# A first unit of 128 rows, the weights split over fewer attention steps, and their sign taken on VectorE instead of GpSimd

## The chip, the cores and the metric

One core of one Trainium2 chip runs the whole program. The time is device microseconds of one launch; the kernel before takes 1611.05 us (median of 3 runs, 1611.02 to 1611.76). The engines are named as in the profile: PE (TensorE matmuls), PEld (its weight loads), DVE (VectorE), ACT (ScalarE), POOL (GpSimd), SP (SyncE, which issues the DMAs here).

## What is computed

Attention with a top-32 mask over 8 batches, 8 heads, 576 positions and a head size of 64, then a gated feed-forward part over the 4608 rows that come out:

```
scores = q @ k^T / 8                       # per batch and head, 576 x 576
kth    = 32nd largest of each row
attn   = softmax of the scores >= kth      # the others are dropped
x      = (attn @ v) as 4608 x 512          # 8 heads of 64 side by side
out    = (sigmoid(x @ w_gate) * (x @ w_val)) @ w_out    # d_ff = 1536
```

q, k and v are 32-bit floats. [...]

## The kernel before, in words

**Attention.** The work is cut into 160 steps. A step (loop variable `n` in `run`) is one tile of 128 query rows for a pair of heads; the last 64 rows of a batch are a narrow step in which the two heads share one tile. So a step has two halves of 128 rows, a narrow one has one: 36 halves a batch, 288 in all. Each half goes through PE (scores, L192), ACT (L199 to SBUF), DVE (`cand`, L257: the 8 largest of each of 8 segments, then four kinds of small operations L261, L263), ACT and POOL (L269, L275: scores under a lead value), DVE (`kths`, L285: the threshold), ACT (L206: exponentials), DVE (L211: mask and sum), PE (L297: transposes into `pt`; `weigh`, L316 to L327: times v). ACT and POOL also split keys, queries and the result (L158, L160, L173, L174, L340, L341) into two parts.

**Groups and units.** `groups` lists the order of the tiles: (batch, first tile, end), each for four pairs of heads. In batch 0 it is tiles 0 and 1 for four pairs (8 steps), tiles 2 and 3 (8 steps), and the 64 rows left (4 steps). `units` lists how the rows are cut for the feed-forward part, as (first row, rows): three units of 256 rows, then ten of 384. A unit may begin when all its rows have come out of the attention; `todo` then gets a generator `ffn` that yields after each piece. A unit runs over three groups of the hidden size (`order`): four pieces of 24 matmuls (`pz`, L369 to L371), then four of 12 (`po2`, L388 to L390; a profile shows it as `po`). That is 432 matmuls a unit whatever its rows, and 18 weight tiles of 1 MB.

**The split of the weights.** 18 weight tiles in 36 halves. Each half (`split_weights`) is loaded (`wraw`, L125), the upper word is scaled on ACT (L132), two POOL instructions multiply the upper word by zero so that only its sign is left (L134), and three DVE instructions (L135, L138, L139) make the high part and the fraction. Then ACT (L140), three matmuls into `wrest` (L141 to L143) and ACT again (L144) make the low part, and L145 stores both to DRAM, from where later units load them. The first unit takes group 1, then 2, then 0, since the tiles of groups 1 and 2 can be used as they are made (`fresh`).

**Pace.** While the split runs, `due` says how many of the 36 halves must have been issued by step `n`: 20 halves over the first `SOON` = 8 steps, then, once the first unit is ready, the other 16 up to step `RUSH` = 15; pieces of the first unit go between them. After that `MILES`, pairs of (attention rows done, feed-forward rows done), sets the pace: at 512 attention rows 256 feed-forward rows, and so on, up to a distance of 448 rows that is kept to the end. Within this a scheduler puts each engine's instructions in order; each engine then runs its own list strictly in order.

## Time and profile before

| what | value |
|---|---|
| median of 3 runs | 1611.05 us |
| the profiled execution | 1610.83 us, of which 1609.0 us are the span of its instructions |
| PE busy | 1541.2 us (96%) |
| DVE, POOL, ACT busy | 1310.4, 1162.1, 1122.6 us |
| HBM read and written | 316.0 and 28.3 MB |

In the 40 slices of the span PE begins with 5778889 and stays at 9 from then on, while DVE and POOL read 7 to 9 in the first seven slices: the start is one stage, with the split in it, the long middle another, and the last three slices, in which DVE reads 2, 0 and 1 and little but feed-forward matmuls is left, a third. PE's busy time is no measure of its speed: matmuls overlap, so their rate has to be read from the distance between their starts.

### The profile page before, as it was taken

The page shows a single profiled execution, that of the slowest core. Times are in us where ns is not written, and L with a number is a line of the kernel's source. Part 1 is how long each engine was busy: PE and PEld are TensorE (multiplying, and loading weights), DVE is VectorE, ACT ScalarE, POOL GpSimd, SP SyncE. Part 2 cuts the span into 40 slices and gives each one's busy share as a digit, 9 for nine tenths or more (in the row PEclk, how much of TensorE's full clock was granted, in tenths as well). Part 3 has the DMA queues.
Part 4 walks back from the last instruction along what each step waited for, and adds up shares of the span by engine and source line. Part 5 has one row for each costly group of instructions (what it writes and reads, how often), then busy time and mean ns, then how long its engine had stood idle before and what let it go on. Part 6 is the DMA issues. An engine that isn't in the chain of part 4 may idle for free.

```text
span 1609.0 us, 34312 instructions
## 1 busy us (share of the span) xinstructions
PE 1541.2 (96%) x10586; PEld 1402.2 (87%) x10586; DVE 1310.4 (81%) x5859; ACT 1122.6 (70%) x2531; POOL 1162.1 (72%) x1871
## 2 busy tenths in 40 slices
PE   5778889999999999999999999999999999999998
PEld 3446669999999999989999999999999999999998
DVE  7999889788998889898888889888988888888201
ACT  7788767677877677777677767678677777767221
POOL 8999998668776886688767876688766887665211
PEclk9789899999999999999999999999999999999999
DMA  7656578777755665565555565566564665554574
GB/s 243 198 175 196 195 253 320 291 273 285 268 185 190 226 233 189 179 234 193 203 207 180 205 235 196 213 213 213 197 219 164 238 215 195 206 200 175 175 281 162
DMA packets 92066, 346.66 MB, mean 215 GB/s; under 512 B 10208, under 2 KB 37344, under 8 KB 63456
## 3 DMA queue, kind: packets, MB, share of 16 engines
q1 hardware_dynamic: 91872, 344.37, 61.7%
q8 instruction: 86, 1.41, 0.4%
q14 instruction: 108, 0.88, 0.2%
HBM read 316.01 MB, written 28.31 MB: 214 GB/s over the span
## 4 chain that ended last, share of the span: by engine, by line
PE 82%; DVE 6%; POOL 4%; ACT 4%; DMA 2%; issue 2%; SPq 0%; POOLq 0%; ACTq 0%; DVEq 0%
PE pz L369 12%; PE pz L370 12%; PE pz L371 12%; PE pss L192 9%; PE po L316 6%; PE pt L297 6%; PE po L388 6%; PE po L389 6%; PE po L390 6%; PE po L318 2%; DMA wraw<-in_w_dram 2%; POOL u L275 2%; DVE cand L257 1%; PE po L327 1%; PE po L321 1%
## 5 line engine op out<-in xcount | busy, mean ns | idle before, releaser
L275 POOL TENSOR_TENSOR u<-s,under 128x288 f32<-128x288 f32 x576 | 454.1, 810 | 108.8 <-ACT under L269 96.1
L257 DVE MAX8 cand<-s 128x8 f32<-128x72 f32 x2304 | 348.8, 218 | 73.3 <-ACT s L199 71.8
L369 PE MATMUL pz<-xh,w 128*128 128x384 f32 (+1 forms) x1184 | 393.4, 333 | 0.7 <-ACT xh L340 0.7
L371 PE MATMUL pz<-xh,w 128*128 128x384 f32 (+1 forms) x1184 | 388.8, 328 | 0.0
L370 PE MATMUL pz<-xl,w 128*128 128x384 f32 (+1 forms) x1184 | 388.3, 328 | 0.4 <-POOL xl L341 0.3
L211 DVE SCALAR_TENSOR_TENSOR e<-s,kths,e 128x576 f32<-128x576 f32 x288 | 281.1, 980 | 10.0 <-ACT e L206 9.8
L269 ACT ACTIVATE under<-s,leads 128x576 bf16<-128x576 f32 x288 | 223.0, 775 | 90.4 <-DVE leads L261 51.0
L285 DVE MAX8 kths<-u 128x8 f32<-128x584 f32 x288 | 218.9, 760 | 39.9 <-POOL u L276 38.6
L377 POOL TENSOR_TENSOR gl<-gf,gh 128x384 fp32r<-128x384 f32 (+1 forms) x156 | 157.6, 1011 | 121.1 <-ACT gh L376 117.3
L206 ACT ACTIVATE e<-s,st 128x576 f32<-128x576 f32 x288 | 209.4, 773 | 28.1 <-POOL st L265 27.9
L369 PEld LDWEIGHTS pz<-xh,w 128*128 128x128 f32 x1184 | 223.0, 189 | 1.9 <-ACT xh L340 1.2
L370 PEld LDWEIGHTS pz<-xl,w 128*128 128x128 f32 x1184 | 223.4, 189 | 0.9 <-POOL xl L341 0.9
L371 PEld LDWEIGHTS pz<-xh,w 128*128 128x128 f32 x1184 | 223.2, 189 | 0.0
L192 PE MATMUL pss<-k,qh 128*128 128x288 f32 (+2 forms) x672 | 198.3, 313 | 23.7 <-ACT s L199 15.3
L199 ACT ACTIVATE s<-pss 128x576 f32<-128x576 f32 x288 | 185.1, 643 | 47.3 <-PE pss L192 42.8
L298 ACT ACTIVATE et<-pt 128x384 f32<-128x384 f32 x384 | 179.0, 487 | 39.8 <-PE pt L297 39.1
L389 PE MATMUL po<-gl,w 128*128 128x384 f32 (+1 forms) x592 | 194.5, 331 | 0.1
L390 PE MATMUL po<-gh,w 128*128 128x384 f32 (+1 forms) x592 | 192.3, 327 | 0.0
L388 PE MATMUL po<-gh,w 128*128 128x384 f32 (+1 forms) x592 | 190.0, 336 | 0.0
L297 PE MATMUL pt<-ident,e 128*128 128x128 f32 x1152 | 180.3, 276 | 7.5 <-DVE e L211 5.3
L192 PE MATMUL pss<-k,ql 128*128 128x288 f32 (+2 forms) x672 | 184.7, 296 | 0.0
L297 PEld LDWEIGHTS pt<-ident,e 128*128 128x128 f32 x1152 | 142.6, 142 | 21.0 <-DVE e L211 8.8
(97 smaller groups left out, 3307.2 us busy)
## 6 DMA issues: line engine op xcount, KB each, us to landing
w<-ws SPq DMA_DIRECT2D x222, 1024.0 KB, 4.9
v<-in_v_dram SPq DMA_DIRECT2D x68, 352.0 KB, 3.9
qraw<-in_q_dram SPq DMA_DIRECT2D x160, 128.0 KB, 3.2
kraw<-in_k_dram SPq DMA_DIRECT2D x64, 288.0 KB, 3.8
wraw<-in_w_dram SPq DMA_DIRECT2D x36, 512.0 KB, 4.4
ws<-w_split SPq DMA_DIRECT2D x36, 512.0 KB, 4.2
out_dram<-acc SPq DMA_DIRECT2D x40, 192.0 KB, 5.0
out_dram<-acc SPq DMA_DIRECT2D x12, 128.0 KB, 5.3
```

Source lines behind the costliest of these rows:

```text
L192: nc.tensor.matmul(ps[:, half, o : o + n], x[:, h * P : (h + 1) * P], ks[h][:, k0 : k0 + n], start=t == 0, stop=t == len(todo) - 1,)
L211: nc.vector.scalar_tensor_tensor(e[:, j], s[:, j], kth[j], e[:, j], op0=ALU.is_ge, op1=ALU.mult, accum_out=st[:, 4 + j : 5 + j])
L257: nc.vector.max(cand[:, j, 8 * g : 8 * g + 8], s[:, j, g * SEG : (g + 1) * SEG])
L269: nc.scalar.activation(under[:, j], s[:, j], AF.Sign, bias=bound, scale=-CUT, accum_out=sums[:, j : j + 1])
L275: nc.gpsimd.tensor_tensor(u[:, j, part], s[:, j, part], under[:, j, part], op=ALU.mult)
L297: nc.tensor.transpose(pt[:, c], ef[:, k0 : k0 + P], ident)
L369: nc.tensor.matmul(ps, wt[:, u, 0, d], xh, start=d == 0, stop=False)
L370: nc.tensor.matmul(ps, wt[:, u, 0, d], xl, start=False, stop=False)
L371: nc.tensor.matmul(ps, wt[:, u, 1, d], xh, start=False, stop=d == NP - 1)
L388: nc.tensor.matmul(ps, wt[:, e % 2, 0, f], gh, start=f == 0, stop=False)
L389: nc.tensor.matmul(ps, wt[:, e % 2, 0, f], gl, start=False, stop=False)
L390: nc.tensor.matmul(ps, wt[:, e % 2, 1, f], gh, start=False, stop=f == FG - 1)
```

## The change

The first unit has 128 rows, the second 256 and all others 384; batch 0 is taken as tile 0 (4 steps), tiles 1 and 2 (8 steps), tile 3 with the 64 rows left (8 steps). `SOON` is 6 and `RUSH` 10, with the line of `due` moved by one step; `MILES` has two entries. In the split the two POOL instructions go; DVE shifts the lead by itself (a new instruction) and then takes the sign bit straight from the upper word. The number of units (13), of matmuls in them and of weight loads stays.

```diff
-    units = [(2 * P * i, 2 * P) for i in range(3)]
-    units += [(t, U) for t in range(2 * U, B * S, U)]
+    units = [(0, P), (P, 2 * P)]
+    units += [(t, U) for t in range(U, B * S, U)]
     halves = {0: ((0, 3), (3, NT + 1)), 1: ((0, 2), (2, NT + 1))}
-    groups = [(0, 0, 2), (0, 2, NT), (0, NT, NT + 1)]
+    groups = [(0, 0, 1), (0, 1, NT - 1), (0, NT - 1, NT + 1)]
...
-    SOON, RUSH = 8, 15
+    SOON, RUSH = 6, 10
...
-    MILES = [(512, 256), (832, 512), (1152, 768), (1536, 1152), (1984, 1536)]
+    MILES = [(384, 128), (832, 384)]
...
                     nc.scalar.activation(lead, sign, AF.Copy, scale=2.0**-112)
-                    for part in (slice(0, 2 * P), slice(2 * P, 4 * P)):
-                        nc.gpsimd.tensor_scalar(sign[:, part], sign[:, part], 0.0, None, op0=ALU.mult)
+                    nc.vector.tensor_scalar(lead_u, lead_u, 3, None, op0=ALU.logical_shift_left)
                     nc.vector.scalar_tensor_tensor(
-                        lead_u, lead_u, 3, top, op0=ALU.logical_shift_left, op1=ALU.bitwise_or
+                        lead_u, top, 0x80000000, lead_u, op0=ALU.bitwise_and, op1=ALU.bitwise_or
                     )
...
-                    due = HELD if not todo else HELD + (2 * n_w - HELD) * (n - SOON) // (RUSH - SOON)
+                    due = HELD if not todo else HELD + (2 * n_w - HELD) * (n + 1 - SOON) // (RUSH - SOON)
```

From the split on every line number is one lower in the changed kernel. The order of the instructions shows what it does to three places.

ACT at the start of the program, before; `wt_lead_0_0` is the first weight half, `s_0_0_0` the first scores:

```order
L158 ACTIVATE k_0_0_1_155<-kraw_0_0_1_153 128x576
L173 ACTIVATE qh_0_1_0_161<-qraw_0_1_0_159 128x256
L132 ACTIVATE wt_lead_0_0_305<-wraw_0_0_303 128x512
L199 ACTIVATE s_0_0_0_177<-pss_0_0_0_0_178 128x576
L132 ACTIVATE wt_lead_0_1_322<-wraw_0_1_320 128x512
```

The same place of the changed kernel:

```order
L157 ACTIVATE k_0_0_1_155<-kraw_0_0_1_153 128x576
L172 ACTIVATE qh_0_0_1_161<-qraw_0_0_1_159 128x256
L198 ACTIVATE s_0_0_0_189<-pss_0_0_0_0_190 128x576
L132 ACTIVATE wt_lead_0_0_319<-wraw_0_0_317 128x512
L172 ACTIVATE qh_0_0_2_179<-qraw_0_0_2_177 128x256
```

The first scores now leave ACT before the first weight half, and no longer behind it.

DVE at the end of the split, before (`17_1` is the last weight half; `kths<-u_0_4_2` and `e_0_4_2` belong to the narrow step of the third pair, `1_0_0` and `1_1_0` to batch 1):

```order
L285 MAX kths_121<-u_0_4_2_3158 128x8
L215 RECIPROCAL st_0_4_1_3056<-st_0_4_1_3056 128x1
L261 MAX tops_1_0_0_3365<-cand_1_0_0_3364 128x8 x2
L394 SCALAR_TENSOR_TENSOR acc_0_1_0_1753<-po2_0_2_0_2627,acc_0_1_0_1753 128x256
L263 MATCH_REPLACE cand_1_0_0_3364<-tops_1_0_0_3365,cand_1_0_0_3364 128x64
L394 SCALAR_TENSOR_TENSOR acc_0_1_1_1768<-po2_0_2_1_2641,acc_0_1_1_1768 128x256
L263 MATCH_REPLACE cand_1_0_0_3364<-tops_1_0_0_3365,cand_1_0_0_3364 128x64
L211 SCALAR_TENSOR_TENSOR e_0_4_2_3157,st_0_4_2_3155<-s_0_4_2_2970,kths_121,e_0_4_2_3157 128x576
L261 MAX tops_1_0_0_3365<-cand_1_0_0_3364 128x8 x2
L135 SCALAR_TENSOR_TENSOR wt_lead_17_1_2675<-wt_lead_17_1_2675,wraw_17_1_2673 128x512
```

The same place of the changed kernel, with the new shift L133:

```order
L284 MAX kths_121<-u_0_4_1_2885 128x8
L332 TENSOR_TENSOR rs_0_2_3_2752<-po_0_2_3_2740,rs_0_2_3_2752 128x256
L138 SCALAR_TENSOR_TENSOR wt_frac_16_1_2044<-wraw_16_1_2041 128x512
L214 RECIPROCAL st_0_3_1_2778<-st_0_3_1_2778 128x2
L260 MAX tops_0_3_2_3032<-cand_0_3_2_3031 128x8
L134 SCALAR_TENSOR_TENSOR wt_lead_17_0_2088<-wraw_17_0_2086,wt_lead_17_0_2088 128x512
L374 SCALAR_TENSOR_TENSOR gf_0_2_3_2019<-gf_0_2_3_2019,pz_0_2_3_1_2006 128x128
L210 SCALAR_TENSOR_TENSOR e_0_4_1_2884,st_0_4_1_2882<-s_0_4_1_2676,kths_121,e_0_4_1_2884 128x576
L133 TENSOR_SCALAR wt_lead_17_1_2104<-wt_lead_17_1_2104 128x512
```

The last half now stands behind fewer attention halves. Counted in the lists up to the last `wt_frac`: 35 of L285 and L211 before and 30 now, 320 of L257 before and 264 now, 113 of L261 and 76 of L263 before and 96 and 64 now.

PE around the last `wrest`, before:

```order
L390 MATMUL po2_0_2_2_2690<-gh_0_2_3_2471,w_split_17_2655 128x256
L142 MATMUL wrest_17_1_2677<-w_split_17_2655,minus_299 128x512
L388 MATMUL po2_0_2_3_2704<-gh_0_2_0_2075,w_split_17_2655 128x256
L389 MATMUL po2_0_2_3_2704<-gl_0_2_0_2076,w_split_17_2655 128x256
L143 MATMUL wrest_17_1_2677<-wt_frac_17_1_2676,plus_298 128x512
L321 MATMUL po_0_4_1_3315<-et_0_4_1_3303,v_2_1_3033 64x64
```

The same place of the changed kernel:

```order
L301 MATMUL pt_0_4_1_0_3240<-ident_105,e_0_4_1_2884 128x128
L140 MATMUL wrest_17_1_2106<-wt_lead_17_1_2104,ident_105 128x512
L141 MATMUL wrest_17_1_2106<-w_split_17_2085,minus_313 128x512
L142 MATMUL wrest_17_1_2106<-wt_frac_17_1_2105,plus_312 128x512
L301 MATMUL pt_0_4_1_0_3240<-ident_105,e_0_4_1_2884 128x128
L387 MATMUL po2_0_2_2_2118<-gh_0_2_0_1601,w_split_17_2085 128x128
```

In both, PE has then done two of the three groups of the first unit but for a few matmuls; that unit has 256 rows before and 128 now.

## Rows read from the trace of the kernel before

**Rows 1.** Windows: stretch, its length, each engine's busy time (instructions), clock, DMA.
```profile
17.00:178.00 161.00, 121.48 (x598) 82.18 (x598) 155.82 (x625) 126.72 (x267) 151.79 (x196) 0.87 0.59 193
178.00:244.00 66.00, 56.60 (x330) 41.90 (x330) 54.98 (x176) 49.40 (x110) 63.42 (x85) 0.91 0.76 248
244.00:300.00 56.00, 56.00 (x481) 52.98 (x480) 48.88 (x240) 39.56 (x97) 40.47 (x76) 0.99 0.85 318
500.00:1500.00 1000.00, 998.68 (x6979) 935.08 (x6977) 857.77 (x3940) 729.02 (x1653) 731.07 (x1219) 1.00 0.59 204
```

**Rows 2.** Waits of DVE from 10 to 178 us: total, times, longest.
```profile
DVE cand L257 <- ACT s L199: 12.7, 3, 10.7
DVE kths L285 <- POOL u L276: 2.2, 2, 1.3
```

**Rows 3.** Waits of DVE from 178 to 244 us.
```profile
DVE cand L257 <- ACT s L199: 3.7, 3, 2.0
DVE kths L285 <- POOL u L276: 2.8, 1, 2.8
DVE rs L333 <- ACT rs L330: 2.6, 1, 2.6
```

**Rows 4.** Timeline around 243 us: start, duration, the last instruction of the split on DVE.
```profile
242.91 1.08 DVE L139 SCALAR_TENSOR_TENSOR wt_frac<-wraw 128x512 fp32r<-128x512 uint32 x1
```

**Rows 5.** Matmul distances: window of 384-row matmuls alone, then timeline with 256 rows.
```profile
1530.00:1590.00 60.00, 60.00 (x345) 59.52 (x345) 7.59 (x14) 12.42 (x25) 10.15 (x10) 1.00 0.74 272
...
249.36 0.28 PE L369 MATMUL pz<-xh,w 128*128 128x256 f32 x1
...
250.56 0.28 PE L370 MATMUL pz<-xl,w 128*128 128x256 f32 x1
```

**Rows 6.** Groups by line from 500 to 1500 us: count, busy us, mean ns, idle before.
```profile
L369 PE MATMUL pz<-xh,w 128*128 128x384 f32 x783 | 269.2, 345 | 0.5 <-ACT xh L340 0.5
...
L389 PE MATMUL po<-gl,w 128*128 128x384 f32 x400 | 136.6, 342 | 0.1
...
L211 DVE SCALAR_TENSOR_TENSOR e<-s,kths,e 128x576 f32<-128x576 f32 x200 | 198.7, 998 | 7.6 <-ACT e L206 7.5
L285 DVE MAX8 kths<-u 128x8 f32<-128x584 f32 x198 | 150.7, 761 | 27.2 <-POOL u L276 26.2
```

**Rows 7.** Groups by line on DVE from 0 to 244 us.
```profile
L257 DVE MAX8 cand<-s 128x8 f32<-128x72 f32 x320 | 49.5, 216 | 16.6 <-ACT s L199 16.4
L211 DVE SCALAR_TENSOR_TENSOR e<-s,kths,e 128x576 f32<-128x576 f32 x35 | 34.4, 987 | 0.0
L135 DVE SCALAR_TENSOR_TENSOR wt_lead<-wt_lead,wraw 128x512 uint32<-128x512 uint32 x36 | 32.1, 893 | 0.8 <-POOL wraw L134 0.8
L139 DVE SCALAR_TENSOR_TENSOR wt_frac<-wraw 128x512 fp32r<-128x512 uint32 x36 | 30.1, 836 | 0.2
L285 DVE MAX8 kths<-u 128x8 f32<-128x584 f32 x35 | 26.5, 757 | 5.2 <-POOL u L276 5.1
L138 DVE TENSOR_SCALAR wraw<-wt_lead 128x512 uint32<-128x512 uint32 x36 | 22.7, 630 | 0.1
L261 DVE MAX8 tops<-cand 128x8 f32<-128x64 f32 x77 | 15.5, 211 | 0.4
```

**Rows 8.** Instructions on `wraw`: count, duration ns min/median/max, first and last start.
```profile
L134 POOL TENSOR_SCALAR wraw<-wraw x72: 872/902/1819, 10.2 to 238.4; 128x256 f32<-128x256 f32 x72
...
L135 DVE SCALAR_TENSOR_TENSOR wt_lead<-wt_lead,wraw x36: 669/886/1283, 14.1 to 240.7; 128x512 uint32<-128x512 uint32 x36
L138 DVE TENSOR_SCALAR wraw<-wt_lead x36: 402/583/1024, 15.0 to 242.0; 128x512 uint32<-128x512 uint32 x36
L139 DVE SCALAR_TENSOR_TENSOR wt_frac<-wraw x36: 667/754/1285, 16.4 to 242.9; 128x512 fp32r<-128x512 uint32 x36
```

**Rows 9.** Timeline of the start: ACT's first weight half and first scores.
```profile
9.43 0.66 ACT L132 ACTIVATE wt_lead<-wraw 128x512 f32<-128x512 f32 x1 [3.45 <-DMA wraw<-in_w_dram]
```

**Rows 10.** Waits of ACT from 0 to 244 us.
```profile
ACT wt_lead L132 <- DMA wraw<-in_w_dram: 15.8, 15, 3.5
```

## What the change should do to the time

> **What bounds the kernel now.** I read the windows by stage first, then the waits, then single groups. From 500 to 1500 us PE is busy for 998.7 of 1000 us and DVE for 857.8; from 244 to 300 us PE is already busy without a gap [rows 1]. So from the moment the weights are split, every microsecond is PE work, and the time is (end of the split) + (PE work still to do then). The split's last DVE instruction ends at 242.91 + 1.08 = 244.0 us [rows 4].
>
> Before that PE is not the limit: it has gaps, and its clock is 0.87 and 0.91 of full [rows 1]. From 17 to 178 us DVE is busy 155.8 of 161 us and POOL 151.8; DVE's real waits in that stretch, apart from the 10.7 us at the program's start, are 2.0 + 2.2 = 4.2 us [rows 2]. DVE sets the pace there. From 178 to 244 us POOL is busy 63.4 of 66 us and DVE only 55.0, and DVE's waits go back to results that others owe it: scores, `u` of POOL, `rs` [rows 1, 3]. There POOL is the fullest engine and DVE loses 11 us. So the stage of 244 us holds 155.8 + 55.0 + about 6 (its part before 17 us, after the 10.7) = 216.9 us of DVE work.
>
> The forecast needs two numbers for the changed kernel: when the split ends, and how much less PE has done by then.
>
> **When the split ends.** DVE's list is strictly in order, so its last split instruction comes no sooner than the work ahead of it. Counted in the lists, there are 56 MAX8 of `cand` less ahead of it (at 49.5 / 320 = 0.155 us, 8.7 us), 5 of L285 and 5 of L211 less (0.757 + 0.987 us each pair, 8.7 us), 29 small operations of 64 columns less (0.21 us as L261, 6 us) [rows 7], and about 3 us less in narrower results (my estimate from eight L333 and eight L375 that halve or shrink). That is 26.4 us. Instructions overlap at their ends: the busy times of all DVE groups of this stretch add up to 253 us for an engine that is busy 216.9, so each price counts 0.86: 23 us.
>
> Added are 36 shifts, one for each half. None is in the trace. The nearest row is L138, also a one-tensor integer operation over 512 columns: 402 to 1024 ns, mean 630 [rows 7, 8]. At the mean it is 36 x 0.630 x 0.86 = 19.5 us; the ends are 12.4 us (all at 402) and 31.7 us (all at 1024). I take the mean. The rewritten L135 reads the same two tensors as before and keeps its price.
>
> The 72 POOL instructions that go (902 ns median [rows 8]) free about 65 us of POOL. POOL had no time left from 178 to 244 us; without them it is no longer the fullest engine. What does that give DVE? First, the 11 us of waits can go. Second, DVE's own instructions may get shorter: L135, L138 and L139 have means of 893, 630 and 836 ns and minima of 669, 402 and 667 [rows 7, 8], so something lengthens them, and POOL is the suspect. From below: nothing is gained, since L211 takes 987 ns on average in the split's stage with POOL 94% busy and 998 ns later with POOL 73% busy [rows 1, 6, 7]. From above: all three fall to their minima, (224 + 228 + 169) ns x 36 x 0.86 = 19 us. L211 is the nearer row, since it shows the same kind of operation at two loads of POOL; but the POOL work that goes is not of the kind that stays. I take 7 us.
>
> The Trainium skill, page "SBUF — State Buffer", section "Who interferes with whom", states a stricter rule: GpSimd and VectorE share one pair of ports under an exclusive lock, and a VectorE instruction with two SBUF inputs, or a one-source one in its two-port mode, waits for the whole of a GpSimd instruction that reads SBUF. By that rule 72 holders of the lock go and the upper end is the right one; that L211 is as long at 73% as at 94% speaks against taking it in full. It is the second rival below.
>
> So DVE's work ahead of the last split instruction is 216.9 - 23 + 19.5 - 7 = 206.4 us. It starts a little earlier: the first scores sat on ACT behind the first weight half, which waited 3.45 us for its DMA and ran from 9.43 us on [rows 9]; now they go first, but DVE's second instruction is a shift that needs that same half. Eight MAX8 come out ahead, 1.2 us: the start is 9.5 us instead of 10.7. Waits: 4.2 us as in the stretch where DVE sets the pace. The split ends at 9.5 + 206.4 + 4.2 = 220.1 us, 23.9 us sooner.
>
> **What PE still has to do.** The rest after the split is larger, and this is what the change pays with. Feed-forward: two thirds of the first unit are done by then, 170.7 rows before and 85.3 now, so 85.3 more rows remain. 345 matmuls of 384 rows take 60 us, 174 ns each; at 256 rows ten distances are 1.20 us, 120 ns each [rows 5]. 432 matmuls of 174 ns for 384 rows are 0.196 us a row: 16.7 us. Narrow matmuls are dearer by the row; of those with 128 rows (66 ns on the line through 120 and 174; no row shows any) only the last third of the unit falls after the split, 144, and they cost about 1 us more than their share. Feed-forward: 17.5 us.
>
> Attention: 5 halves fewer have passed DVE. From 500 to 1500 us there are 198 halves and about 3 x 783 + 3 x 400 = 3549 feed-forward matmuls [rows 6]; at 174 ns these take 618 us, which leaves 382 us, or 1.93 us of PE for a half. PE's own list has a little more than 5 halves less in scores, transposes and products, in all 11 us.
>
> Nothing else changes in the PE-bound part: the same 13 units, the same matmuls, the same distance of 448 rows at the end and so the same tail. One risk was that DVE bounds the next stretch, since `MILES` lets only 256 feed-forward rows go with 448 attention rows. But up to 832 rows there are then 22 halves left, 22 x 1.93 + 10 + 52 (last third of the first unit, and 432 x 120 ns) = 104 us of PE, against 22 x 857.8 / 198 = 95 us of DVE [rows 1, 6]. PE stays the limit, by a tenth.
>
> **Sum.** -23.9 + 17.5 + 11 = +4.6 us on the profiled execution's 1610.83 us, which is within 0.3 us of the median 1611.05: 1615.4, rounded to 1615 us. The shorter split is worth nearly as much as it costs; the sign of the result hangs on DVE's prices.
>
> **Rivals.**
> Forecast, 1615 us, its own range 1609 to 1623 (shift between 402 and 800 ns, relief between 3 and 10 us): the split ends near 220 us with DVE full. Chance 0.63.
>
> DVE runs free, 1596 us: without the POOL instructions the three old split operations fall to their minima (19 us instead of 7) and the shift costs 402 ns (7 us less), so the split ends at 201 us. For it: the minima exist, and POOL is full in the whole stage [rows 1, 8]. Against: L211 is no shorter with POOL at 73% [rows 6, 7], and `u`, keys and queries stay on POOL. Chance 0.22.
>
> The split gets a new wait, 1631 us, slower: 36 halves in ten steps instead of 15 ask more of the chain DMA, ACT, DVE for each half with three raw buffers; ACT already waits 15.8 us for `wraw` in 15 places [rows 10]. If DVE then idles in the second half of the split as it did from 178 to 244 us (11 of 66 us, so 18 us in 110) in place of 2 us, the split ends at 236 us. It decides as soon as a raw half lands later than DVE reaches its shift. Against: the load's buffer comes free at L139, several us of other DVE work before the next half. Chance 0.15.
>
> **How the numbers follow.** A measurement of this kernel can tell 0.2%, 3.2 us, from no change, so "same" is 1607.8 to 1614.3. The forecast's own range gives some 0.05 faster, 0.20 same and 0.38 slower; the free DVE counts as faster but for 0.02, the new wait as slower: faster 0.25, same 0.22, slower 0.53. The range from 1601 to 1631 holds the forecast and half of each rival.
>
> **What would show it.** In the profile after: the last `wt_frac` at about 220 us; PE without gaps right after it; DVE over 95% busy from 17 us to there, with next to no waits for POOL; POOL at 60 to 70% there; 30 of L285 by then; the shift near 0.6 us and L135, L138, L139 a little shorter; the same rate of halves from 500 us on, and an equal tail. I am wrong if the split ends before 214 us (faster) or after 232 us, if L135 or L211 fall near their minima, or if PE shows gaps after the split, since then the rest is not PE's.

## The result, and the profile after

The changed kernel takes 1631.8 us (median of 4 runs, 1630.1 to 1633.0) against 1611.4 us for the kernel before on the same chip: ratio 1.0128 (1.0113 to 1.0143), 20 us slower. Its profiled execution is 1631.1 us, with a span of 1628.9 against 1609.0 us.

The windows of the four stretches of [rows 1], in the kernel after:

```profile
17.00:178.00 161.00, 129.38 (x607) 91.09 (x607) 152.22 (x587) 124.03 (x265) 102.19 (x143) 0.80 0.63 211
178.00:244.00 66.00, 63.46 (x460) 53.41 (x456) 60.62 (x233) 48.46 (x114) 50.45 (x77) 0.92 0.83 293
244.00:300.00 56.00, 56.00 (x493) 52.97 (x493) 38.71 (x184) 36.28 (x88) 29.69 (x54) 1.00 0.78 286
500.00:1500.00 1000.00, 1000.00 (x6970) 937.21 (x6967) 848.98 (x3943) 730.95 (x1652) 729.11 (x1218) 1.00 0.59 205
```

POOL falls from 151.8 to 102.2 and from 63.4 to 50.5 us, and PE bounds the long middle as before. The last split instruction on DVE, the counterpart of [rows 4], in the timeline:

```profile
216.62 1.19 DVE L138 SCALAR_TENSOR_TENSOR wt_frac<-wraw 128x512 fp32r<-128x512 uint32 x1
```

It ends at 217.8 us; 220.1 was predicted, 244.0 was it before. On PE the split's last matmul, in the timelines of after and of before:

```profile
223.74 0.40 PE L142 MATMUL wrest<-wt_frac,plus 128*128 128x512 f32 x1
```

```profile
246.28 0.40 PE L143 MATMUL wrest<-wt_frac,plus 128*128 128x512 f32 x1
```

So PE leaves the split at 224.1 instead of 246.7 us, 22.5 us sooner, and yet the kernel is slower: what is left to do then takes 42.5 us more. The groups of DVE from 0 to 244 us, which answer to [rows 7]; L133 is the new shift:

```profile
L256 DVE MAX8 cand<-s 128x8 f32<-128x72 f32 x296 | 46.6, 218 | 8.1 <-ACT s L198 8.1
L210 DVE SCALAR_TENSOR_TENSOR e<-s,kths,e 128x576 f32<-128x576 f32 x35 | 32.8, 940 | 0.0
L138 DVE SCALAR_TENSOR_TENSOR wt_frac<-wraw 128x512 fp32r<-128x512 uint32 x36 | 29.8, 829 | 0.3
L134 DVE SCALAR_TENSOR_TENSOR wt_lead<-wraw,wt_lead 128x512 uint32<-128x512 uint32 x36 | 28.9, 804 | 0.1
...
L133 DVE TENSOR_SCALAR wt_lead<-wt_lead 128x512 uint32<-128x512 uint32 x36 | 19.8, 553 | 6.3 <-ACT wt_lead L132 6.2
L137 DVE TENSOR_SCALAR wraw<-wt_lead 128x512 uint32<-128x512 uint32 x36 | 18.5, 517 | 0.1
```

The means of the three old operations are lower than before, L134 by 89 ns, L137 by 113, L138 by 7, and still far from the minima. Their medians are not (count, duration ns min/median/max; 886, 583 and 754 before [rows 8]):

```profile
L134 DVE SCALAR_TENSOR_TENSOR wt_lead<-wraw,wt_lead x36: 668/690/1287, 10.8 to 212.1; 128x512 uint32<-128x512 uint32 x36
L137 DVE TENSOR_SCALAR wraw<-wt_lead x36: 406/428/1018, 13.3 to 215.0; 128x512 uint32<-128x512 uint32 x36
L138 DVE SCALAR_TENSOR_TENSOR wt_frac<-wraw x36: 666/688/1289, 14.6 to 216.6; 128x512 fp32r<-128x512 uint32 x36
```

So most of them run near the minimum, and some take nearly twice as long. Now the matmuls of the first unit, in the timeline of PE; first a piece after the split, then one inside it (start, duration):

```profile
228.20 0.28 PE L368 MATMUL pz<-xh,w 128*128 128x128 f32 x1
228.31 0.27 PE L369 MATMUL pz<-xl,w 128*128 128x128 f32 x1
228.43 0.27 PE L370 MATMUL pz<-xh,w 128*128 128x128 f32 x1
...
229.54 0.30 PE L296 MATMUL pt<-ident,e 128*128 128x128 f32 x1
```

```profile
130.07 0.41 PE L368 MATMUL pz<-xh,w_split 128*128 128x128 f32 x1
130.29 0.41 PE L369 MATMUL pz<-xl,w_split 128*128 128x128 f32 x1
130.50 0.41 PE L370 MATMUL pz<-xh,w_split 128*128 128x128 f32 x1
```

From 228.20 to 229.54 us there are 12 distances of 112 ns; the median over such stretches is 111 ns. The prediction had 66. A matmul of 128 rows costs nearly as much as one of 256, 120 ns [rows 5]. Inside the split the distance is 213 ns. Windows of smaller stretches show the clock there, and where else PE loses time:

```profile
100.00:120.00 20.00, 14.78 (x69) 8.38 (x68) 20.00 (x79) 17.43 (x37) 12.26 (x19) 0.93 0.58 191
120.00:140.00 20.00, 19.52 (x84) 18.22 (x84) 20.00 (x86) 13.45 (x32) 11.64 (x18) 0.50 0.51 165
140.00:160.00 20.00, 20.00 (x89) 14.36 (x89) 14.76 (x48) 7.44 (x17) 9.75 (x16) 0.67 0.38 121
160.00:180.00 20.00, 20.00 (x133) 15.74 (x132) 18.87 (x63) 19.39 (x43) 13.64 (x18) 1.00 0.78 252
...
330.00:360.00 30.00, 26.45 (x185) 21.72 (x181) 27.13 (x134) 23.16 (x53) 25.05 (x44) 1.00 0.54 173
```

From 120 to 140 us the granted clock is 0.50, the level of 1.2 GHz, with PE busy for 19.5 of 20 us; from 140 to 160 us PE is the limit, and DVE has 5 us of gaps in a stretch that should be DVE's. From 330 to 360 us it is the other way round: PE has gaps of 3.5 us at full clock, in what the prediction took for PE-bound. From 300 to 500 us they are 5.0 us; before, 1.4:

```profile
300.00:500.00 200.00, 194.96 (x1372) 177.90 (x1372) 177.09 (x842) 151.21 (x344) 152.73 (x254) 1.00 0.60 207
```

```profile
300.00:500.00 200.00, 198.61 (x1578) 185.61 (x1578) 170.88 (x815) 147.09 (x347) 145.87 (x253) 1.00 0.71 252
```

(after, then before). From 224 us to the end of the program the gaps are 5.0 us, before 2.7 from 246.7 us on.

### The profile page after: what moved, and what is told of

The parts are those of the page before. It is cut to its first block, busy times and chain, and to the rows that moved or that the text cites. A ratio compares the mean times of both kernels' runs of the same rounds, so it can differ in the third digit from the quotient of the medians.

```text
span 1628.9 us, 34375 instructions
## 1 busy us (share of the span) xinstructions
PE 1574.1 (97%) x10658; PEld 1434.8 (88%) x10658; DVE 1315.0 (81%) x5899; ACT 1130.1 (69%) x2539; POOL 1098.2 (67%) x1803
## 4 chain that ended last, share of the span: by engine, by line
PE 76%; POOL 1%; DVE 1%; ACT 0%; issue 0%; POOLq 0%; ACTq 0%
PE pz L369 11%; PE pz L370 11%; PE pz L368 11%; PE pss L191 8%; PE pt L296 6%; PE po L315 6%; PE po L387 6%; PE po L388 5%; PE po L389 5%; PE po L317 2%; PE po L326 1%; PE po L320 1%; PE pt L301 1%; POOL u L274 1%; PE po L322 0%
## 5 line engine op out<-in xcount | busy, mean ns | idle before, releaser
L368 PE MATMUL pz<-xh,w 128*128 128x384 f32 (+2 forms) x1184 | 399.9, 338 | 0.0
L370 PE MATMUL pz<-xh,w 128*128 128x384 f32 (+2 forms) x1184 | 394.2, 333 | 0.0
L369 PE MATMUL pz<-xl,w 128*128 128x384 f32 (+2 forms) x1184 | 392.8, 332 | 0.7 <-POOL xl L340 0.7
L210 DVE SCALAR_TENSOR_TENSOR e<-s,kths,e 128x576 f32<-128x576 f32 x288 | 277.3, 967 | 0.2
L376 POOL TENSOR_TENSOR gl<-gf,gh 128x384 fp32r<-128x384 f32 (+2 forms) x156 | 154.9, 994 | 112.9 <-ACT gh L375 108.9
L198 ACT ACTIVATE s<-pss 128x576 f32<-128x576 f32 x288 | 184.6, 641 | 39.6 <-PE pss L191 38.7
L387 PE MATMUL po<-gh,w 128*128 128x384 f32 (+2 forms) x592 | 195.6, 342 | 1.0 <-DVE acc L393 0.8
L388 PE MATMUL po<-gl,w 128*128 128x384 f32 (+2 forms) x592 | 196.0, 334 | 0.0
L389 PE MATMUL po<-gh,w 128*128 128x384 f32 (+2 forms) x592 | 194.9, 332 | 0.0
```

The costliest lines, as they stand in the source:

```text
L210: nc.vector.scalar_tensor_tensor(e[:, j], s[:, j], kth[j], e[:, j], op0=ALU.is_ge, op1=ALU.mult, accum_out=st[:, 4 + j : 5 + j])
L368: nc.tensor.matmul(ps, wt[:, u, 0, d], xh, start=d == 0, stop=False)
L369: nc.tensor.matmul(ps, wt[:, u, 0, d], xl, start=False, stop=False)
L370: nc.tensor.matmul(ps, wt[:, u, 1, d], xh, start=False, stop=d == NP - 1)
L387: nc.tensor.matmul(ps, wt[:, e % 2, 0, f], gh, start=f == 0, stop=False)
L388: nc.tensor.matmul(ps, wt[:, e % 2, 0, f], gl, start=False, stop=False)
```

## The experiments

Every ratio is to the kernel before on the same chip. It takes 1610.1 to 1611.4 us on the chips used, so a difference between the times of two other kernels is good to about 2 us. Unless said otherwise an edit is against the changed kernel.

The table divides the span of some of the kernels, in us. Each PE instruction after PE has left the split counts from its start to the start of the next one; idle time stands apart as gaps.

| kernel | PE leaves the split at | feed-forward | attention | gaps | span |
|---|---|---|---|---|---|
| before | 246.7 | 914.0 | 445.6 | 2.7 | 1609.0 |
| changed | 224.1 | 941.6 | 458.2 | 5.0 | 1628.9 |
| experiment 1 ("kernel 1") | 232.0 | 917.3 | 445.1 | 4.9 | 1599.2 |
| experiment 2 | 240.4 | 955.3 | 455.5 | 4.1 | 1655.3 |
| experiment 5 | 220.8 | 963.2 | 454.5 | 0.9 | 1639.4 |
| experiment 6 | 224.0 | 966.8 | 458.5 | 4.6 | 1653.8 |
| experiment 9 | 237.9 | 934.4 | 454.1 | 11.5 | 1637.9 |
| experiment 10 | 269.2 | 897.6 | 440.7 | 10.1 | 1617.7 |

**1. The new split alone.** The kernel before with only the four lines of the split changed.

```diff
-                    for part in (slice(0, 2 * P), slice(2 * P, 4 * P)):
-                        nc.gpsimd.tensor_scalar(sign[:, part], sign[:, part], 0.0, None, op0=ALU.mult)
+                    nc.vector.tensor_scalar(lead_u, lead_u, 3, None, op0=ALU.logical_shift_left)
...
```

> The kernel before with the new split alone (shift and sign on VectorE, no GpSimd), old units, groups and pace. Theory A (the narrow unit is what costs): the shift adds some 17 us to VectorE up to the end of the split, shorter split operations and the waits for GpSimd from 178 to 244 us give back 10 to 18 us, the split ends between 240 and 248 us, and the time is 1607 to 1615 us, no change that 0.2% can tell. Rival B (the work moved to VectorE is what costs): VectorE is the limit of the whole split and gets nothing back, the split ends at 255 us or later, and the time is 1622 us or more.

1601.1 us, 0.9945 (0.9928 to 0.9962): faster than either theory said. Windows of this kernel:

```profile
17.00:178.00 161.00, 127.24 (x617) 86.54 (x618) 158.93 (x636) 130.34 (x275) 105.80 (x148) 0.86 0.61 199
...
178.00:244.00 66.00, 56.94 (x390) 45.00 (x389) 64.31 (x226) 51.17 (x115) 55.80 (x80) 0.97 0.83 278
...
300.00:500.00 200.00, 198.31 (x1569) 184.88 (x1569) 178.76 (x858) 154.23 (x359) 152.53 (x260) 1.00 0.69 242
```

DVE has 36 shifts more (20.6 us) and is done with the split at 229.1 instead of 244.0 us, with 34 halves of attention done by then instead of 35: it is busy 64.3 instead of 55.0 of the 66 us from 178 on [rows 1]. Up to the last split instruction DVE is busy for 217.3 us, before for 216.9; but after its first instruction it idles 2.5 us instead of 16.4. What GpSimd's 72 instructions cost was above all VectorE's waits.

**2. The rest alone.** The changed kernel with the old split on GpSimd (the same lines, the other way).

> The changed kernel with the old split: two GpSimd instructions a half, no shift on VectorE; units of 128, 256, 384 rows and the new pace stay. Theory A: the narrow unit is still there, so the time stays well above before; GpSimd is full again, and the split ends at 225 to 235 us instead of 218, so the time is 1635 to 1645 us. Rival B (the new split costs the time): without the shift VectorE has 17 us less to do, and the time falls back to 1615 us or less.

1658.8 us (1641.4 to 1663.5), 1.0277 (1.0209 to 1.0344). Units and pace without the new split lose more than the whole change, and the split gains in both surroundings. Neither theory goes as high; the split ends on DVE at 237.4 us, later than the first one said. Windows here:

```profile
240.00:260.00 20.00, 20.00 (x97) 19.24 (x97) 12.95 (x66) 6.92 (x19) 10.58 (x21) 0.50 0.47 172
260.00:300.00 40.00, 40.00 (x258) 38.30 (x258) 9.92 (x35) 9.76 (x27) 10.66 (x21) 0.69 0.67 237
```

Behind the split PE is full here at a granted clock of 0.50 and 0.69, while DVE is busy for 13 of 20 and 10 of 40 us. In the changed kernel the clock is 1.00 there. The 154 narrow matmuls that are left take 33 us, in the changed kernel 168 take 20.

**3. GpSimd back in every second half** (against kernel 1).

```diff
+                    if i == 0:
                         nc.vector.tensor_scalar(lead_u, lead_u, 3, None, op0=ALU.logical_shift_left)
...
+                    else:
+                        for part in (slice(0, 2 * P), slice(2 * P, 4 * P)):
+                            nc.gpsimd.tensor_scalar(sign[:, part], sign[:, part], 0.0, None, op0=ALU.mult)
...
```

> Old units, groups and pace; every first half takes the new split (shift on VectorE), every second half the old one (two GpSimd instructions). VectorE then has 18 shifts less, some 9 us, than with the new split alone (1601 us, split ends at 229 us), and GpSimd some 32 us more, which still leaves it room. If VectorE's list alone sets the end of the split: it ends at 220 to 224 us and the time is 1592 to 1597 us. Rival (GpSimd's instructions lengthen VectorE's by as much as is saved): 229 to 234 us, and 1601 to 1606 us.

1609.2 us, 0.9986 (0.9977 to 0.9996): 8 us worse than kernel 1, with 18 shifts fewer on DVE, and worse than the rival too. Its last split instruction in the timeline, and its window:

```profile
236.68 0.67 DVE L145 SCALAR_TENSOR_TENSOR wt_frac<-wraw 128x512 fp32r<-128x512 uint32 x1
```

```profile
178.00:244.00 66.00, 55.71 (x353) 44.24 (x353) 59.96 (x214) 50.67 (x114) 61.00 (x81) 0.95 0.76 247
```

The split ends 8.2 us later than in kernel 1, with one half of attention more done by then (35, some 4 us of DVE), and DVE has 4.4 us more gaps from 178 to 244 us, with POOL at 61 of 66 us. That GpSimd's instructions lengthen the stage is shown.

**4. The pace: `MILES`, `SOON` and `RUSH`, then all of it** (with `RUSH` 14).

```diff
-    MILES = [(384, 128), (832, 384)]
+    MILES = [(384, 128), (832, 384), (1152, 768), (1536, 1152), (1984, 1536)]
```

> The changed kernel, but after 832 attention rows the pace of the kernel before (768 feed-forward rows at 1152, 1152 at 1536, 1536 at 1984) instead of a distance of 448 rows at once. Theory A: the 5 us in which PE is idle between 300 and 500 us come from the pace, since feed-forward matmuls are held back there; they go, and the time is 1625 to 1628 us. Rival: PE waits there for the attention itself (masks of VectorE, products of GpSimd), the gaps only move, and the time stays within 3 us of 1631.

```diff
-    SOON, RUSH = 6, 10
+    SOON, RUSH = 8, 15
```

> The changed kernel with the pace of the split from before (20 halves over 8 steps, the rest up to step 15); units of 128, 256, 384 rows, groups and new split stay. Theory A (the narrow unit costs): most of the loss stays, 1618 to 1632 us. Rival B (the shorter pace costs): the time falls to 1601 to 1610 us, near the 1601 us of the new split with old units and pace.

```diff
-    SOON, RUSH = 6, 10
+    SOON, RUSH = 8, 14
-    MILES = [(384, 128), (832, 384)]
+    MILES = [(512, 256), (832, 512), (1152, 768), (1536, 1152), (1984, 1536)]
-                    due = HELD if not todo else HELD + (2 * n_w - HELD) * (n + 1 - SOON) // (RUSH - SOON)
+                    due = HELD if not todo else HELD + (2 * n_w - HELD) * (n - SOON) // (RUSH - SOON)
```

> The changed kernel (new split, first unit of 128 rows) with all of the pace of before: SOON 8, RUSH 14 and the five MILES. Theory A (the pace is not the cause: alone, its two parts made the changed kernel 5 us slower each): 1632 to 1642 us. Rival (the two parts of the pace belong together, and the new one costs the 11 us that the narrow unit does not): 1618 to 1624 us.

1636.5 us, 1.0163 (1.0146 to 1.0180); 1637.0 us, 1.0152 (1.0135 to 1.0169); 1657.6 us, 1.0281 (1.0217 to 1.0346). The old pace is worse in every form, and worst in full, each time beyond what either theory gave. The new pace is not the cause of the loss; with this narrow unit the old one costs 5 us in each part and 26 us in full. In both runs with the old pace of the split PE is full from 240 to 260 us at a granted clock of 0.50, with DVE busy for 6 of 20 us, as in experiment 2.

**5. A second narrow unit.** The third unit, 384 rows, cut into 128 and 256.

```diff
-    units += [(t, U) for t in range(U, B * S, U)]
+    units += [(3 * P, P), (4 * P, 2 * P)]
+    units += [(t, U) for t in range(2 * U, B * S, U)]
```

> The changed kernel with the third unit (384 rows) cut into 128 and 256: a second unit of 128 rows, all of it after the split, where every microsecond is PE work. 432 matmuls of 128 rows and 432 of 256 take the place of 432 of 384. Theory A (a matmul of 128 rows takes as long as its weight load, 111 ns): 48.0 + 51.8 - 75.2 = 24.6 us more, so 1652 to 1660 us. Rival (66 ns, on the line through 120 ns at 256 rows and 174 ns at 384, as the prediction had it): 28.5 + 51.8 - 75.2 = 5.1 us more, so 1634 to 1640 us.

1643.6 us, 1.0215 (1.0195 to 1.0235), 12 us over the changed kernel: between the two. Its matmuls of 128 rows are 111 ns apart, and feed-forward takes 21.6 us more (table), near theory A. But PE has hardly any gaps from 300 to 500 us (0.7 instead of 5.0 us), the split ends 3.3 us sooner on PE, and attention takes 3.7 us less. The place was not clean.

**6. The last unit cut** into 256 and 128 rows, where PE has little else to do.

```diff
+    units[-1:] = [(B * S - U, 2 * P), (B * S - P, P)]
```

> The changed kernel with its last unit of 384 rows cut into 256 and 128, in the stretch in which PE has little but feed-forward matmuls left. Theory A (a matmul of 128 rows costs 111 ns, one of 256 rows 120, one of 384 rows 174, and all of it is paid where PE is the limit): 432 x (0.111 + 0.120 - 0.174) = 24.6 us more, 1656 us (1653 to 1659). Theory B (the prediction's line through 120 and 174 down to 66 ns; the 111 ns come from something at the start of the program): 432 x 0.012 = 5.2 us more, 1637 us (1635 to 1639).

1656.0 us, 1.0288 (1.0270 to 1.0305): 24.2 us more, where theory A had 24.6. In the table feed-forward takes 25.2 us more and the rest is as in the changed kernel. The last unit in the timeline:

```profile
1630.44 0.27 PE L389 MATMUL po<-gl,w 128*128 128x128 f32 x1
1630.55 0.27 PE L390 MATMUL po<-gh,w 128*128 128x128 f32 x1
1630.66 0.28 PE L388 MATMUL po<-gh,w 128*128 128x128 f32 x1
```

Where PE is the limit the 111 ns are paid in full. The granted clock is 1.00 from 1600 to 1650 us.

**7. A lean first unit**: of the three products with a weight (high x high, high x low, low x high) only the first, 144 instead of 432 narrow matmuls; two thirds of that unit's products are left out.

```diff
...
-                        nc.tensor.matmul(ps, wt[:, u, 0, d], xl, start=False, stop=False)
-                        nc.tensor.matmul(ps, wt[:, u, 1, d], xh, start=False, stop=d == NP - 1)
+                        if n > P:
+                            nc.tensor.matmul(ps, wt[:, u, 0, d], xl, start=False, stop=False)
+                            nc.tensor.matmul(ps, wt[:, u, 1, d], xh, start=False, stop=d == NP - 1)
...
```

> The changed kernel, but the first unit (128 rows) takes only the product high x high: 144 matmuls of 128 rows instead of 432, the others left out. Theory A, strong form (the narrow unit is PE's limit inside the split too, where the trace of the changed kernel shows PE full from 120 to 180 us at a clock of 0.5 to 0.67): some 20 us inside the split and 96 x 0.111 = 11 us behind it go, so 1598 to 1606 us. Weak form (inside the split PE is hidden behind VectorE): only the 11 us behind the split go, 1619 to 1624 us. Rival B (the shorter pace is what costs, not the unit): 1627 us or more.

1613.3 us, 1.0017 (1.0008 to 1.0027): 18.5 us under the changed kernel, between the two forms of theory A; rival B is out. The 288 matmuls are 32 us at 111 ns; a part of them lies beside DVE's work in the split. Clock from 120 to 160 us: 0.76 and 0.93.

**8. The same matmuls twice as wide.** The first unit takes its 128 columns twice; the copy is not used.

```diff
+        twice = n == P
...
+        def wide(x):
+            return x.unsqueeze(1).to_broadcast([P, 2, P]) if twice else x
...
-                        nc.tensor.matmul(ps, wt[:, u, 0, d], xh, start=d == 0, stop=False)
+                        nc.tensor.matmul(to, wt[:, u, 0, d], wide(xh), start=d == 0, stop=False)
...
```

> The changed kernel, but the 432 matmuls of the first unit take their 128 columns twice (256 columns; the second copy is not used). Theory A (narrow matmuls cost their weight load, 111 ns, and besides bring the granted clock down where they run back to back): the clock from 120 to 160 us is above 0.85 instead of 0.50 and 0.67, the matmuls there are 120 to 140 ns apart instead of 213, the time is 1620 to 1628 us although PE does twice the columns. Theory B (the clock falls there for another reason, and only the distance counts): the clock stays at 0.5 to 0.7, the distance grows from 111 to 120 ns at full clock and from 213 to about 240 ns at the low one, and the time is 1636 to 1641 us (432 x 9 ns = 4 us, and some 200 x 27 ns = 5 us).

1632.7 us, 1.0138 (1.0121 to 1.0155): within the changed kernel's interval. Of theory A the clock came true, the time did not:

```profile
120.00:140.00 20.00, 20.00 (x137) 17.75 (x137) 20.00 (x90) 16.55 (x39) 12.69 (x21) 0.86 0.52 176
140.00:160.00 20.00, 18.92 (x122) 14.64 (x121) 20.00 (x70) 16.48 (x39) 17.52 (x24) 1.00 0.55 184
```

With distances of 120 ns and DVE full again, the whole is as long as before. The clock has to be read in finer windows, first of the changed kernel, then of this one:

```profile
126.00:153.00 27.00, 27.00 (x109) 23.20 (x109) 25.25 (x100) 15.01 (x36) 19.19 (x29) 0.50 0.34 107
```

```profile
126.00:153.00 27.00, 26.41 (x189) 22.58 (x188) 27.00 (x115) 23.79 (x57) 22.25 (x30) 1.00 0.55 183
```

From 110 to 119 us the clock is 1.00 and 0.99 with PE busy for 4.0 and 5.4 of 9 us, and from 119 to 126 us it is 0.50 and 0.53: it falls at the same place in both kernels. With 128 columns it stays at 0.50 up to 153 us, with 256 columns it is back at 1.00 from 126 us on. Narrow matmuls do not always go with the low clock: behind the split they run at 1.00 in the changed kernel (224 to 244 us), and so they do in experiment 6.

Nor is the low clock where the 20 us went: with 432 x 9 ns = 4 us more of PE's work and the same time, it was worth some 3 us here. That is an estimate, since the order moved too: the split ends at 225.4 us with 33 halves done, in the changed kernel at 217.8 with 30.

**9. The narrow unit second**, with the pace of before (against kernel 1).

```diff
-    units = [(2 * P * i, 2 * P) for i in range(3)]
-    units += [(t, U) for t in range(2 * U, B * S, U)]
+    units = [(0, 2 * P), (2 * P, P)]
+    units += [(t, U) for t in range(U, B * S, U)]
-    groups = [(0, 0, 2), (0, 2, NT), (0, NT, NT + 1)]
+    groups = [(0, 0, 2), (0, 2, NT - 1), (0, NT - 1, NT + 1)]
-    SOON, RUSH = 8, 15
+    SOON, RUSH = 8, 14
```

> The new split and the pace of before, first unit of 256 rows after 8 steps as before; only the second unit has 128 rows and all others 384 (the groups of batch 0 follow: tile 2 alone, then tile 3 with the 64 rows left; RUSH 14). Theory A (the time is PE's work plus idle time; the cut 256, 128, 384 in place of 256, 256, 256 is 432 x (0.111 + 0.174 - 0.240) = 19.4 us more work): 1601 + 19.4 = 1620.5 us (1617 to 1624), so that of the 31 us between the split alone and the changed kernel 19 belong to the narrow unit wherever it stands and 11 to its being first and to the pace. Rival (the narrow unit costs because it is the first one, inside the split): 1601 to 1608 us.

1639.5 us, 1.0179 (1.0161 to 1.0198): 38 us over kernel 1, more than either theory. The windows show 12 us of gaps on PE in two places, one behind the split and one at its end, where kernel 1 has next to none:

```profile
320.00:360.00 40.00, 34.16 (x257) 29.13 (x257) 36.83 (x187) 32.75 (x77) 27.53 (x51) 1.00 0.47 162
220.00:240.00 20.00, 14.22 (x79) 11.19 (x80) 20.00 (x100) 10.95 (x25) 10.38 (x17) 0.91 0.81 279
```

The rival, that the unit costs because it is first, is out. Theory A's 19.4 us of work are not all. In the table PE leaves the split 5.9 us later than in kernel 1, and then feed-forward takes 17.1 us more, attention 9.0 and gaps 6.6. In both early places tried, more is lost around the narrow unit than its price; the groups and the pace go with it, and no run parts them.

**10. Twelve units of 384 rows** (against kernel 1), the least work for PE and the latest first unit.

```diff
-    units = [(2 * P * i, 2 * P) for i in range(3)]
-    units += [(t, U) for t in range(2 * U, B * S, U)]
+    units = [(t, U) for t in range(0, B * S, U)]
-    groups = [(0, 0, 2), (0, 2, NT), (0, NT, NT + 1)]
+    groups = [(0, 0, 3), (0, 3, NT + 1)]
-    SOON, RUSH = 8, 15
+    SOON, RUSH = 12, 19
```

> The new split with twelve units of 384 rows in place of three of 256 and ten of 384; the first unit is ready after 12 steps, and SOON and RUSH are 12 and 19. Theory A (the time is PE's work plus idle time that the units do not touch): 12 x 432 x 0.174 = 902.0 us of feed-forward matmuls instead of 3 x 432 x 0.120 + 10 x 432 x 0.174 = 907.2, so 1596 us (1592 to 1600). Rival (a later first unit leaves PE without feed-forward work for four steps more, and what PE lacks then it never gets back): PE's gaps up to the split's end grow by some 20 us, 1612 to 1622 us.

1618.8 us, 1.0054 (1.0037 to 1.0070), 17.7 us over kernel 1. The time is the rival's, its reason is not: up to its last matmul of the split PE idles 55.9 us, in kernel 1 51.9, so 4 us more and not 20. Of the operations on `wraw` (count, duration ns min/median/max, first and last start) the last begins at 263.6 us, 35 us later than in kernel 1 (228.5):

```profile
L137 DVE SCALAR_TENSOR_TENSOR wt_frac<-wraw x36: 665/679/1283, 13.0 to 263.6; 128x512 fp32r<-128x512 uint32 x36
```

PE leaves the split 37 us later than in kernel 1, and the feed-forward that is left then is only 20 us shorter (table). So the saving of wide units is lost before the split ends; which step loses it stays open. Of the three first units tried, 128, 256 and 384 rows, each with its pace, 256 is the best.

**11. The sign on ScalarE** (against kernel 1): it multiplies the upper word of each 64-bit weight by 0.0, and the shift joins the old operation.

```diff
-                    nc.vector.tensor_scalar(lead_u, lead_u, 3, None, op0=ALU.logical_shift_left)
+                    nc.scalar.activation(sign, sign, AF.Copy, scale=0.0)
...
-                        lead_u, top, 0x80000000, lead_u, op0=ALU.bitwise_and, op1=ALU.bitwise_or
+                        lead_u, lead_u, 3, top, op0=ALU.logical_shift_left, op1=ALU.bitwise_or
```

> Old units, groups and pace; the sign comes from one ScalarE instruction that multiplies the upper word by zero, VectorE has no shift of its own and GpSimd no part. VectorE has 36 shifts less (about 17 us), ScalarE 36 x 0.57 = 20 us more on top of some 80% busy. If VectorE's list alone sets the end of the split: it ends at 212 to 218 us and the time is 1586 to 1593 us. Rival (ScalarE gets full and scores, exponentials and weight halves queue on it): the split ends at 230 us or later, and the time is 1602 us or more.

1596.4 us, 0.9908 (0.9891 to 0.9925). The output is the one that the absolute values of the weights give: the zero comes out without its sign, and this kernel leaves the sign of the weights out. The time lies between theory and rival, and the split ends late, as the rival had it (230.5 us). Then with a bias of -0.0 as a constant (`bias=-0.0`), and read from SBUF (`AF.Identity, bias=negz`):

> The run in which ScalarE makes the sign by a multiplication by 0.0, now with a bias of -0.0, so that the sign stays and no part of the computation is left out. Theory: the bias costs nothing, since it is a constant of the same instruction: 1596 us (1592 to 1600), below the kernel before by some 0.9%. Rival: the instruction with a bias is longer than without; at twice its duration 36 x 0.6 = 22 us more on ScalarE, which is 92% busy from 60 to 120 us: 1605 to 1615 us.

> The run with the sign on ScalarE, the bias of -0.0 now read from a column of 128 values in SBUF instead of a constant of the instruction. Theory A (as cheap as with the constant): 1596 us (1592 to 1600). Rival (a bias from SBUF makes the 36 instructions longer): 1602 us or more.

1597.4 us, 0.9913 (0.9896 to 0.9930), and 1605.3 us, 0.9972 (0.9962 to 0.9982). Contrary to the first expectation both give the same output as without the bias, so the sign is still lost, and these are prices of an operation, not versions to use. The two forms in their traces:

```profile
L133 ACT ACTIVATE wraw<-wraw x36: 651/673/777, 10.6 to 219.0; 128x512 f32<-128x512 f32 x36
```

```profile
L135 ACT ACTIVATE wraw<-wraw,negz x36: 752/774/833, 10.6 to 222.3; 128x512 f32<-128x512 f32 x36
```

With 36 shifts fewer on DVE the gain over kernel 1 is some 4 us; the split ends no sooner (230.3 against 229.1 us), but with 36 halves of attention done instead of 34. The form with the bias from SBUF, which has the function Identity in place of Copy, takes 101 ns longer each. Its time is 8 us longer, which 36 x 0.101 = 3.6 us do not give, and its split ends sooner (227.5 us); how the 8 us come about is not shown.

**12. A shorter split by `RUSH` alone** (the kernel with the constant bias, RUSH 15 to 11).

> The run with the sign on ScalarE (with its bias) and all units as before, but RUSH 11 instead of 15: the split is issued in fewer attention steps. Theory A (up to the split's end VectorE's list sets the time, so an earlier end only moves attention work behind it): the last split instruction some 12 us sooner (218 us instead of 230), and the time within 5 us of the run with RUSH 15. Rival (an earlier end is worth its microseconds, since PE has no gap afterwards): 1584 to 1590 us. Rival on the other side (the first unit's matmuls then crowd the same stretch and PE or ScalarE becomes the limit): 1603 us or more.

1596.4 us, 0.9916 (0.9900 to 0.9933). The time is theory A's, but it tells nothing apart: the last split instruction ends at 230.9 us, not at 218 (230.3 with RUSH 15). `RUSH` alone does not bring the late halves forward there.

## Why the prediction was wrong, step by step

**The split's end was right.** 217.8 us against 220.1. The shift took 553 ns on average against 630, so 17 instead of 19.5 us. The relief of the old operations was (89 + 113 + 7) ns x 36 x 0.86 = 6.5 us, with L210 (47 ns x 35 x 0.86) 8 us, against 7. The stricter rule, of the Trainium skill's page "SBUF — State Buffer", section "Who interferes with whom", would have made it 19 us; this trace shows less than half. That POOL lengthens these operations, the prediction's suspicion, is shown: 38 of the 144 instructions L133, L134, L137 and L138 overlap no POOL instruction, and none of these takes over 452 (L133, L137) or 698 ns (L134, L138). But POOL still has other work beside most of them. L135 near its minimum was one of the prediction's signs of being wrong; it came for the median (690 ns, minimum 668) and not for the mean. Waits were larger: from 10 to 218 us, DVE's waits in the kernel after are

```profile
DVE wt_lead L133 <- ACT wt_lead L132: 6.2, 3, 3.8
DVE kths L284 <- POOL u L275: 1.9, 2, 1.2
DVE st L214 <- POOL st L213: 1.6, 3, 0.7
```

9.7 us against 4.2. The longest, 3.8 us, ends at 160.7 us, behind the stretch at the low clock. So the hit holds some luck: DVE began at 8.1 us instead of 9.5, was busy for 199.1 us instead of 206.4, and idled 10.6 us instead of 4.2, and these errors nearly cancel. PE followed DVE's end by 6.3 us, 2.7 before, and left the split 22.5 us sooner, where 23.9 was predicted for both.

**What PE still had to do was not.** Predicted: 17.5 + 11 = 28.5 us more. Measured on the profiled executions: (1628.9 - 224.1) - (1609.0 - 246.7) = 42.5 us, which with the sooner end makes up the 19.9 us of the spans' difference. By the table of the experiments the 42.5 us are 27.6 of feed-forward, 12.6 of attention and 2.3 of gaps. The mechanism of the prediction holds, an earlier end paid for with more PE work; the term that was wrong is feed-forward, 27.6 us instead of 17.5.

**The step that failed** is the price of a narrow matmul in that term: "those with 128 rows (66 ns on the line through 120 and 174; no row shows any) [...] cost about 1 us more than their share". Two points were drawn out into a range where something else sets the distance. There was a row of that width: the transposes of attention. In the timeline of PE before:

```profile
240.77 0.49 PE L302 MATMUL pt<-ident,e 128*128 128x128 f32 x3
241.10 0.27 PE L305 MATMUL pt<-ident,e 128*64 128x128 f32 x1
```

Three distances are 0.33 us, 110 ns each; the median over the transposes from 500 to 1500 us is 109 ns. At 111 ns, and with the 264 narrow matmuls that had run by 224.1 us (278 of 256 rows by 246.7 us before), feed-forward left is 168 x 0.111 + 432 x 0.120 + 11 x 432 x 0.174 = 897.3 us against 154 x 0.120 + 2 x 432 x 0.120 + 10 x 432 x 0.174 = 873.8: 23.5 us more. The 168 narrow matmuls at 111 instead of 66 ns are 7.6 us of that. (By the prediction's own distances, with 144 matmuls of the first unit left in both, the term is 15.6 us; 17.5 leaves out that one unit of 256 rows fewer comes after.) The 4 us up to 27.6 are distances longer than these, where one piece of work follows another: over all its matmuls of 384 rows the mean is 182 ns in both kernels, and the changed one has 432 more of them left. In the whole program it is plainer still. By the line, 66 + 120 + 174 = 3 x 120, and so the cut into 128, 256 and 384 rows seemed free; measured, it is 432 x (0.111 + 0.120 + 0.174 - 0.360) = 19.4 us of PE's work. Experiment 6 shows that such microseconds come out one for one where PE is the limit.

The Trainium skill, page "TensorE: Matmul & The Clock Gate", section "LDWEIGHTS (loading the stationary operand)", puts a weight load at its columns over 1.2 ns, 107 ns for 128 columns, and the 111 ns agree with a distance that the load sets. The Trainium skill, same page, section "Back-to-back issue gap", gives about 81 ns for 128 rows; no trace here shows that, and the measurement decides.

**The second miss** is "PE stays the limit, by a tenth", for the stretch up to 832 rows. PE's gaps from 300 to 500 us grew from 1.4 to 5.0 us, one of the prediction's own signs of being wrong; over all that is left after the split it is 2.3 us. A reading that fits, though no run isolates it: while the narrow unit and the second one fill PE, DVE runs short (38.7 us busy of 56 from 244 to 300 us, 48.9 before [rows 1]), and PE then waits for the attention that DVE did not do. Experiments 2 and 9 show both halves of this, larger.

**Attention** was nearly right: 5 halves fewer had passed when the split ended, as counted, and they are 12.6 us of PE's time against 11. "The same matmuls" holds for feed-forward; in attention, tile 0 taken alone makes 144 products of 128 columns where 72 of 256 were.

**The rivals.** The time is by chance that of the new wait, 1631 us, but its mechanism did not come: that put the split's end at 236 us, and ACT waited less for `wraw` than before (13.2 us against 15.8 [rows 10]). "DVE runs free" did not happen in full, but the direction it named is real: the split without GpSimd is worth 10 us by itself (experiments 1 and 3).

**The change as a whole:** 1611 - 10 for the split, + 19.4 for narrow matmuls, + 11 lost around the narrow unit = 1631 us. The last term is what remains between kernel 1 and the changed kernel. By the table it is not gaps: the changed kernel leaves the split 7.9 us sooner than kernel 1 and then has 24.3 us more of feed-forward, 13.1 more of attention and 0.1 of gaps. So it lies in work that was not done when the split ended, in which the low clock and the 3.8 us wait of DVE may have a part; no run divides it further. Kernel 1, the new split with the old units and pace, beats both kernels at 1601.1 us.

## What to carry to other kernels

Before cutting work into narrower matmuls, find a row of that width, a transpose of the same width if nothing else (the trace before had one, at 109 ns), since the price does not fall in proportion: here 384, 256 and 128 rows cost 174, 120 and 111 ns. Price what remains after a stage with the same care as the stage itself. And try the parts of a change apart: here one part gained 10 us and the other lost 31.

## What the hardware showed that was not expected

- Matmuls of 128 rows back to back are 111 ns apart at a granted clock of 1.00 and 213 ns at 0.50. At 0.50 those of 256 rows in the kernel before are as far apart: 212 ns from 244.03 to 245.09 us, against 120 at 1.00.
- PE can be full for long at the low clock: with 128 rows the granted clock was 0.50 from 126 to 153 us with PE busy for all of the 27 us, after a stretch with gaps (4.0 of 9 us busy from 110 to 119 us). The same data taken twice, 256 columns, ran at 1.00 in the same place. Behind the split matmuls of 128 rows ran at 1.00.
- ScalarE's copy with a scale of 0.0 gives a zero without the sign, and a bias of -0.0, constant or from SBUF, does not bring it back (experiment 11: the output of all three is that of the absolute weights).
- 72 small GpSimd instructions delayed VectorE more by what it had to wait for than by longer instructions: up to the end of the split DVE is busy for 217.3 us in kernel 1, which has 36 instructions more and one half of attention less, and for 216.9 before, but idles 2.5 us instead of 16.4 after its first instruction.
- DVE's split operations were near their minimum whenever no POOL instruction overlapped them, and up to nearly twice as long when one did (L134: at most 693 against 1287 ns).
